# A new order for the start and the first pair of a hashed attention with two expert layers behind it

## The chip, the cores and the metric

The kernel runs on one core of a Trainium2 chip. The metric is the device time of one execution in microseconds (us). TensorE (PE) has two levels of clock here, 1.2 and 2.4 GHz. The other engines are VectorE (DVE), ScalarE (ACT), GpSimd (POOL) and SyncE, whose queue (SP) issues nearly all DMAs.

## The reference

All arrays are float32. An attention over 2 batches, 8 heads, 768 tokens and head dimension 64 keeps only the keys whose hash bucket equals the query's; a soft mixture of 8 experts follows, and then a layer of 2048 hidden units.

```python
q_bits = (np.einsum('bhsd,dk->bhsk', q, proj) > 0)      # 6 bits, a bucket of 0..63; k the same
mask = q_bucket[:, :, :, None] == k_bucket[:, :, None, :]
scores = np.where(mask, scale * np.matmul(q, k.transpose(0, 1, 3, 2)), -1e9)
scores = scores - np.max(scores, axis=-1, keepdims=True)
attn = np.exp(scores); attn = attn / (np.sum(attn, -1, keepdims=True) + 1e-9)
x = np.matmul(attn, v)                                  # heads joined: 1536 tokens x 512
...
logits = x @ phi                                        # 32 slots: dispatch over tokens, 8 experts, combine
...
h = x @ w_in; g = h - np.tanh(h); out = g @ w_out
```

## The kernel before, in words

Two heads make a pair, and there are eight pairs. The work of a pair is cut into small units, and each unit issues a few instructions on several engines. Every engine takes its instructions strictly in the order in which the units are written out, so the lists of unit names below are the schedule. `START` (line 66) is the order of what comes ahead of the first pair; `STEP` (line 71) is gone through once for each of pairs 0 to 6, `LAST` (line 74) for pair 7. In `START` a name carries its pair after the dot. In a step of pair i, the table `role` (line 678) adds an offset: `m`, `l`, `g`, `f`, `d`, `v` and `v1`, `v2` work on pair i+1, `h`, `b` on pair i+2, `qk` on i+3, the score units `s0`, `s1` and `a` on pair i itself.

The units that matter here:

- `const.0`, `const.1`, `const.2` load constants: `ct` on the SP queue; the small `blk` on SP and the hash matrix `projb` on ACT's queue; `phiB` in two DMAs on SP. `qk` loads a pair's queries and keys (xq, xk), `v` its values (tv).
- `bq`, `bk` (lines 349 to 357): the hash bits of queries or keys, matrix products `pb` on PE and comparisons `bt` on DVE. `wq0v`, `wk0a`, `wq1p` and so on (line 359) write rows made of the bits beside the operands QA, KA; the last letter says the engine (v DVE, a ACT, p POOL, s a part on ACT and a part on DVE).
- `h0` to `h3` (`hp` on POOL): the rounded high part of keys and queries into KA, QA. `l0` to `l3`: the low part into KB, QB. For pair 0 the low parts are subtractions on POOL (lines 426 to 433). For later pairs `g` copies the high part to PSUM on ACT (line 407, tile hp) and `l` subtracts it on DVE (line 416). `d` copies the high parts into the other halves of QB, KB by DMA.
- `m` (line 437), 18 for a pair: masked scores `pm` on PE, and the maximum over keys of them on DVE (`mx`, line 446). `fa`, `fb` (one head each) and `f2` (both) transpose the maxima (`mh`, `pc` on PE, `zrow`, `row` on DVE) and send them by DMA into QA; `fz` sends the flags of empty rows (zrw).
- `s0`, `s1` (line 497), nine for each head: the scores `pst` on PE (line 503), the exponential `e` on ACT (line 505), and for most a running sum `es` on POOL (line 515). `a` (line 520) is the product of `e` of both heads and the values, `pav` on PE.
- `v1`, `v2`: sums of the values (va on POOL, pv on PE, vt on DVE, vhi on ACT, vn and vzw on POOL).
- `wl`, `wc` (lines 629, 638): load a piece of the third layer's weight and convert it: one `cg` on ACT and three operations on DVE (lines 183, 192, 197, the middle one needs `cg`). At most two pieces are loaded and not converted; a `wc` with nothing loaded does nothing.
- `keep.n` and `warm.4`: small products on PE whose results nobody uses. `oi` clears rows of operands (on POOL, and once on DVE).

PSUM tiles of all these units come from one pool of six, `ps` (line 270).

After the pairs, the expert layer's weights stream in on SP as buffers come free (`load_pieces`, called at fixed places of pairs 5 to 7), and the last layer follows in an order of its own (`MOE`, `RUN`, `LOOP`).

Of the kernel before, what the change touches and what calls it, by code (L numbers as in the profile page):

```python
# [25 lines left out]
NPR = B * H // 2  # L26
# [36 lines left out]

START = ("warm.4 const.1 qk.0 const.0 hp2.0 keep.1 oi.0 const.2 h0.0 bk.0 bq.0 keep.3 wq0v.0 kc.0 wl.0 keep.3 wk0a.0 "
# [3 lines left out]
        "keep.1 oi.2 wl.0").split()  # L70
STEP = ("a a a m xe s0 g1 m a m l1 s1 s0 s1 m s0 m m g0 l0 m xr s1 h1 m m s0 m a m m wl m g2 s1 lp l2 s0 v wl a d m wc "
        "lp v1 e m s0 s0 a wl a lp a e s1 lp m m h0 s1 s0 qk m v2 h3 s1 e lp a f2 lp b s0 x2 e fz wc s1 wc s1 lg lp h2 "
        "x3 a a wl lp").split()
LAST = ("a a s0 a lp xe a a a s0 lp lp a a lp s0 s0 lp s0 s1 s1 s0 s1 xr s0 s1 s1 lp s1 s1 lp a a lp a s0 x2 s1 s0 lg "
        "x3 s1 a").split()
# [57 lines left out]
def body(ctx: ExitStack, tc: tile.TileContext, q, k, v, proj, phi, w1, w2, w_in, w_out, cst, out, dbg=None):  # L133
    nc = tc.nc
    const = ctx.enter_context(tc.tile_pool(name="const", bufs=1))
# [6 lines left out]
    lg = const.tile([P, B * KT, NS], F32, name="lg")  # L142
# [78 lines left out]
    def open_ring(n, stack, side="right"):  # L221
        for _ in range(n):
            slots.append(stack.enter_context(tc.tile_pool(name=f"ring{len(slots)}", bufs=1, side=side, reuse_waits="tile")))
# [10 lines left out]
    def load_pieces(n):  # L234
        for _ in range(n):
            t = n_loaded[0]
            if t >= NPC or t >= len(slots) < NSLOT:
                return
            n_loaded[0] += 1
            which, e, half = pieces[t]  # L240
            w = slot_tile(slot_of(t), F32R if which == 4 else F32, "w")
            if which != 4:
                src = w_out.bitcast(U32)[e] if which == 3 else (w1, w2)[which - 1][e, half]
                nc.sync.dma_start(out=w.rearrange("p a n -> p (a n)").bitcast(src.dtype), in_=src)
            w_t[pieces[t]] = w


    def attention():
# [31 lines left out]
        last = NPR - 1  # L280
# [348 lines left out]
        def win_load():  # L629
            n = win_n[0]  # L630
            if n < 16 and len(raws) < 2:
                win_n[0] += 1
                c, fq = n // 4, n % 4
                raw = cv.tile([P, 1024], U32, tag="raw", name="raw")
                nc.sync.dma_start(out=raw, in_=win_v[:, c, fq * 1024:(fq + 1) * 1024])
                raws.append((raw, c, fq))

        def win_cvt():
            if raws:
                raw, c, fq = raws.pop(0)  # L640
                g = cv.tile([P, 512], F32, tag="cg", name="cg")
                l = psum("cl")[:, :512].bitcast(U32)
                cvt_b(cvt_a(raw, g, l), win[:, c, fq * 512:(fq + 1) * 512])
# [96 lines left out]
        nc.vector.memset(wz, 0.0)  # L740
        for w in START:
            u, n = w.split(".")
            unit(u, int(n))
        del wt[:]
        for i in range(NPR):
            for u in STEP if i < NPR - 1 else LAST:
                n = i + role.get(u, role.get(u[0], 0))
                if 0 <= n < NPR:
                    unit(u, n)
                if i == 5 and not slots and 6 not in xqs and 6 not in xks:  # L750
                    while raws or win_n[0] < 16:
                        win_load()
                        win_cvt()
                    raw_x.close()
                    open_ring(RING[0], rctx)
                if i == 6 and len(slots) == sum(RING[:2]) and not xqs and not xks:
                    xq_x.close()
                    open_ring(RING[2], rctx)
                if i == last and half.get((i, 0)) == len(SEQ) and len(slots) == sum(RING[:4]) and not xtu and last in pav:
                    head_x.close()  # L760
                    load_pieces(RING[3])
                    open_ring(RING[4], rctx)
                    load_pieces(RING[4])
                if i == last and half.get((i, 1)) == len(SEQ) and len(slots) == sum(RING[:5]):
                    last_x.close()
                    open_ring(RING[5], rctx)
                    load_pieces(RING[5])
            if i == 5:
                mid_x.close()
                open_ring(RING[1], rctx)  # L770
            if i == 6:
                early_x.close()
                load_pieces(RING[1] + RING[2])
                open_ring(RING[3], rctx)
        last = NPR - 1
# [549 lines left out]

    with tc.manual_schedule():
        attention()
        if dbg is not None and "lg" in dbg:
            nc.sync.dma_start(out=dbg["lg"], in_=lg)
# [70 lines left out]
```

## Time and profile before

| what | us |
|---|---|
| runs of the kernel, lowest, median, highest | 464.77, 465.33, 466.93 |
| the profiled execution, its time | 464.5 |
| its span, first to last instruction | 462.7 |
| busy: PE, DVE, ACT, POOL | 442.7, 330.5, 271.8, 289.3 |

The time of an execution holds 1.8 us outside the span. Busy PE counts matmuls whose ends are modelled, and the products of `keep` too. The order of the units is read off on each engine: an idle time that a row names belongs to the instruction that comes next in the list.

### The profile page before, as it was taken

The page shows a single profiled execution, that of the slowest core. Times are in us where ns is not written, and L with a number is a line of the kernel's source. Part 1 is how long each engine was busy: PE and PEld are TensorE (multiplying, and loading weights), DVE is VectorE, ACT ScalarE, POOL GpSimd, SP SyncE. Part 2 cuts the span into 40 slices and gives each one's busy share as a digit, 9 for nine tenths or more (in the row PEclk, how much of TensorE's full clock was granted, in tenths as well). Part 3 has the DMA queues.
Part 4 walks back from the last instruction along what each step waited for, and adds up shares of the span by engine and source line. Part 5 has one row for each costly group of instructions (what it writes and reads, how often), then busy time and mean ns, then how long its engine had stood idle before and what let it go on. Part 6 is the DMA issues. An engine that isn't in the chain of part 4 may idle for free. (4 is left out here: it accounts for less than half of the span.)

```text
span 462.7 us, 7587 instructions
## 1 busy us (share of the span) xinstructions
PE 442.7 (96%) x2639; PEld 296.6 (64%) x2639; DVE 330.5 (71%) x592; ACT 271.8 (59%) x521; POOL 289.3 (63%) x291
## 2 busy tenths in 40 slices
PE   7589999999999999999999999999999999999995
PEld 3455565656666575766765544567777778888883
DVE  3999798897989969577173438579998976544441
ACT  4526676756776565654450111278889887666661
POOL 4976977889697896958871110025888884444450
PEclk9889999999999999999999999999999999999998
DMA  6337337153633509449539999992000003000004
GB/s 195 110 98 221 125 98 219 41 170 127 189 125 106 167 15 298 178 142 326 216 157 379 421 416 417 419 419 83 2 1 2 0 0 137 1 1 1 0 1 144
DMA packets 18342, 71.32 MB, mean 154 GB/s; under 512 B 3668, under 2 KB 4792, under 8 KB 13176
## 3 DMA queue, kind: packets, MB, share of 16 engines
q1 hardware_dynamic: 17976, 70.75, 43.5%
q8 instruction: 23, 0.38, 0.4%
q14 instruction: 23, 0.19, 0.1%
q10 hardware_dynamic: 320, 0.01, 0.0%
HBM read 60.08 MB, written 3.15 MB: 137 GB/s over the span
## 5 line engine op out<-in xcount | busy, mean ns | idle before, releaser
L505 ACT ACTIVATE e<-pst 128x512 f32<-128x512 f32 x144 | 79.9, 598 | 44.6 <-PE pst L503 40.9
L515 POOL TENSOR_TENSOR es<-es,e 128x512 f32<-128x512 f32 x73 | 92.9, 1288 | 13.1 <-ACT e L505 13.0
L446 DVE TENSOR_REDUCE mx<-pm 128x1 f32<-128x512 f32 x144 | 90.2, 682 | 10.7 <-PE pm L444 9.8
L532 PE MATMUL pav<-e,tv 128*64 128x512 f32 (+1 forms) x384 | 70.5, 496 | 0.0
L503 PE MATMUL pst<-QA,KA 128*128 128x256 f32 (+1 forms) x192 | 67.7, 367 | 0.8 <-DVE mx L446 0.4
L503 PE MATMUL pst<-QB,KB 128*128 128x256 f32 (+1 forms) x192 | 62.2, 338 | 0.0
L1221 DVE SCALAR_TENSOR_TENSOR ph<-win,ph 128x512 f32<-128x512 f32 (+1 forms) x64 | 35.7, 558 | 32.2 <-ACT win L1216 30.8
L444 PE MATMUL pm<-KA,QA 96*128 96x512 f32 x192 | 51.5, 369 | 2.8 <-DVE QA L368 2.4
L1252 POOL TENSOR_TENSOR split<-win,split 128x512 fp32r<-128x512 f32 x31 | 44.8, 1447 | 14.2 <-ACT split L1247 14.2
L1273 PE MATMUL po<-w,split 128*128 128x512 f32 x128 | 51.0, 399 | 0.0
L1271 PE MATMUL po<-w,split 128*128 128x512 f32 x128 | 50.6, 396 | 0.0
L515 POOL TENSOR_TENSOR es<-e 128x512 f32<-128x512 f32 x30 | 39.2, 1316 | 18.1 <-PE pr L546 18.0
L1272 PE MATMUL po<-w,split 128*128 128x512 f32 x128 | 50.5, 394 | 0.0
L444 PEld LDWEIGHTS pm<-KA,QA 96*128 96x128 f32 x192 | 34.0, 197 | 24.1 <-ACT e L505 7.3
L503 PEld LDWEIGHTS pst<-QA,KA 128*128 128x128 f32 x192 | 36.1, 188 | 20.2 <-DVE mx L446 7.1
L1252 POOL TENSOR_TENSOR ghl<-win,ghl 128x256 fp32r<-128x256 f32 x32 | 24.2, 757 | 37.0 <-ACT ghl L1247 37.0
L1216 ACT ACTIVATE win<-ph 128x512 f32<-128x512 f32 (+1 forms) x64 | 30.8, 481 | 23.0 <-PE ph L1209 22.3
L1222 DVE SCALAR_TENSOR_TENSOR win<-win,ph 128x512 f32<-128x512 f32 (+1 forms) x64 | 35.5, 555 | 8.7 <-DVE ph L1221 0.5
L532 PEld LDWEIGHTS pav<-e,tv 128*64 128x64 f32 x384 | 24.1, 136 | 27.1 <-issue 20.4
L1217 ACT ACTIVATE win<-win,ct 128x512 f32<-128x512 f32 (+1 forms) x64 | 39.5, 617 | 2.1
L503 PEld LDWEIGHTS pst<-QB,KB 128*128 128x128 f32 x192 | 36.4, 189 | 2.0
L1273 PEld LDWEIGHTS po<-w,split 128*128 128x128 f32 x128 | 24.0, 188 | 7.7 <-POOL split L1252 2.7
(236 smaller groups left out, 818.4 us busy)
## 6 DMA issues: line engine op xcount, KB each, us to landing
w<-in_moe_w_dram SPq DMA_DIRECT2D x32, 1024.0 KB
raw<-in_moe_w_in_dram SPq DMA_DIRECT2D x16, 512.0 KB
w<-in_moe_w_out_dram SPq DMA_DIRECT2D x8, 1024.0 KB
xq<-in_q_dram SPq DMA_DIRECT2D x8, 384.0 KB
xk<-in_k_dram SPq DMA_DIRECT2D x8, 384.0 KB
tv<-in_v_dram SPq DMA_DIRECT2D x8, 384.0 KB
out_dram<-win SPq DMA_DIRECT2D x12, 256.0 KB
QB<-QA SPq DMA_DIRECT2D x10, 192.0 KB
```

What stands on the lines that cost most here:

```text
L444: nc.tensor.matmul(pm[:, j * 256:j * 256 + c1 - c0], QA[s][h][:96, c * P:(c + 1) * P], KA[s][h][:96, c0:c1], start=True, stop=True)
L446: nc.vector.reduce_max(m, pm.rearrange("p (c k) -> p c k", c=len(cs)), axis=AX.X)
L503: nc.tensor.matmul(pst[:, j * 256:j * 256 + c1 - c0], K[h][:, c * P:(c + 1) * P], Q[h][:, c0:c1], start=x == 0, stop=x == 1)
L505: nc.scalar.activation(e, pst, AF.Exp, scale=0.125)
L515: eng.tensor_tensor(q[0], y, e, ALU.add)
L532: nc.tensor.matmul(pav[i][k][64 * h:64 * h + 64, :], tv[i][:, h, c, :], e2[h][:, j * 256:j * 256 + c1 - c0], start=False, stop=c == KT - 1 ...
L1217: nc.scalar.activation(w, z, AF.Square, bias=ct[:, C_QA:C_QA + 1])
L1221: nc.vector.scalar_tensor_tensor(self.ph[p], z, Q_C, self.ph[p], ALU.mult, ALU.mult)
L1252: (eng or nc.gpsimd).tensor_tensor(gl[p], g, gh[p].bitcast(F32), ALU.subtract)
L1271: nc.tensor.matmul(po, gh[p][:, us], wo.half(f, 0), start=f == 0, stop=False)
L1272: nc.tensor.matmul(po, gh[p][:, us], wo.half(f, 1), start=False, stop=False)
L1273: nc.tensor.matmul(po, gl[p][:, us], wo.half(f, 0), start=False, stop=f == NF - 1)
```

## The change

Three things are edited, all of them orders. `START` is a new list. It holds the old one's units and six `s0.0`, the first six score units of the first head of pair 0, near its end; there are 9 products of `keep` fewer (14 for 23). The first pair goes through a list of its own, `FIRST`, which is `STEP` with six `s0` fewer and another order.

```diff
-START = ("warm.4 const.1 qk.0 const.0 hp2.0 keep.1 oi.0 const.2 h0.0 bk.0 bq.0 keep.3 wq0v.0 kc.0 wl.0 keep.3 wk0a.0 "
-        "h1.0 wq1a.0 keep.1 qk.1 keep.1 hp3.0 wl.0 m.0 m.0 m.0 keep.1 m.0 m.0 m.0 wk1a.0 m.0 m.0 m.0 h3.1 h2.1 h1.1 "
-        "v.0 fa.0 m.0 m.0 m.0 m.0 l1.0 m.0 m.0 m.0 oi.1 m.0 m.0 wl.0 keep.1 keep.3 v.1 v1.0 wc.0 bq.1 d.0 bk.1 l0.0 "
-        "fb.0 l2.0 l3.0 h0.1 wq1p.1 wq0p.1 v2.0 keep.3 wk0v.1 fz.0 keep.3 keep.2 kc.1 a.0 qk.2 wc.0 wc.0 wk1a.1 "
-        "keep.1 oi.2 wl.0").split()
+START = ("qk.0 warm.4 const.0 const.2 const.1 wl.0 hp2.0 oi.0 bk.0 keep.1 h0.0 wl.0 keep.3 keep.3 bq.0 kc.0 wq0v.0 "
+        "wk0a.0 h1.0 keep.1 hp3.0 m.0 keep.1 m.0 qk.1 v.0 m.0 m.0 m.0 wk1a.0 h1.1 wq1a.0 keep.1 m.0 m.0 h3.1 m.0 d.0 "
+        "h2.1 m.0 m.0 m.0 fa.0 m.0 m.0 m.0 l1.0 m.0 m.0 m.0 oi.1 l0.0 m.0 keep.1 wl.0 v.1 keep.3 l3.0 bq.1 v1.0 bk.1 "
+        "wq1p.1 wc.0 wq0p.1 v2.0 s0.0 fb.0 l2.0 wk0v.1 h0.1 s0.0 wc.0 s0.0 a.0 s0.0 wc.0 oi.2 wl.0 s0.0 fz.0 wk1a.1 "
+        "kc.1 s0.0 qk.2").split()
+FIRST = ("a g1 a m m a m l1 xe a s1 xr m s1 m m m g0 m h1 s1 l0 a m m wl v1 m m d m g2 l2 a s1 v lp wl m h0 a lp wc a wl "
+        "lp e m s0 a m qk lp m s1 e s0 s1 m s0 v2 h3 s1 lp f2 e lp b a fz wc s1 s1 lg lp e x3 h2 a a wl x2 lp wc").split()
 STEP = ("a a a m xe s0 g1 m a m l1 s1 s0 s1 m s0 m m g0 l0 m xr s1 h1 m m s0 m a m m wl m g2 s1 lp l2 s0 v wl a d m wc "
         "lp v1 e m s0 s0 a wl a lp a e s1 lp m m h0 s1 s0 qk m v2 h3 s1 e lp a f2 lp b s0 x2 e fz wc s1 wc s1 lg lp h2 "
         "x3 a a wl lp").split()
...
-            for u in STEP if i < NPR - 1 else LAST:
+            for u in FIRST if i == 0 else STEP if i < last else LAST:
```

A unit whose pair does not exist, an `a` without both exponentials, and a `wc` or `wl` that has nothing to do issue nothing. The effective changes of order in `START` are these. The loads of xq, xk go ahead of `blk`, and two pieces of weight go ahead of `qk.1`. `bk.0` stands ahead of the first `keep`. `fa.0` stands behind eleven `m.0` and not nine, `d.0` ahead of it. Behind the last `m.0`, both hash units `bq.1`, `bk.1` stand ahead of the first `wc` and not behind it; then come `v2.0`, the first `s0.0` and `fb.0`, which was ahead of `v2.0`. On ACT the order behind `vhi` (of `v2.0`) is now: e, h0.1, e, cg, e, e, e, the rows of `wk1a.1`, e, and then `g1.1` of the first pair. It was: cg, `wk1a.1`, e, `g1.1`.

## Rows read from the trace of the kernel before

**Rows 1.** Busy time of each engine in stretches: the start, steps 0 and 1.
```profile
8.20:34.85 26.65, 18.44 (x92) 12.71 (x90) 23.89 (x44) 11.14 (x18) 21.41 (x25) 0.87 0.41 131
34.85:60.27 25.42, 24.43 (x129) 14.22 (x130) 22.80 (x42) 17.71 (x32) 21.54 (x21) 1.00 0.54 160
60.27:87.83 27.56, 27.56 (x167) 17.18 (x166) 24.76 (x47) 18.57 (x34) 22.34 (x22) 1.00 0.48 137
```
**Rows 2.** The timeline of DVE, start of the kernel to the first pair.
```profile
11.27 2.36 DVE L368 TENSOR_SCALAR QA<-bt,ct 24x512 fp32r<-24x512 f32 x2
...
26.11 0.68 DVE L183 TENSOR_SCALAR cl<-raw 128x512 uint32<-128x512 uint32 x1
...
28.34 1.97 DVE L357 TENSOR_SCALAR bt<-pb 24x512 f32<-24x512 f32 x4
30.32 0.17 DVE L451 TENSOR_REDUCE mh<-mx 128x6 f32<-128x12 f32 x1
...
31.46 0.27 DVE L490 TENSOR_TENSOR vt<-pv,blk 4x128 f32<-4x128 f32 x1
31.77 0.91 DVE L368 TENSOR_SCALAR KA<-bt,ct 24x512 fp32r<-24x512 f32 x2
...
34.85 1.88 DVE L446 TENSOR_REDUCE mx<-pm 128x1 f32<-128x512 f32 x3
36.64 1.37 DVE L416 TENSOR_TENSOR QB<-xq,hp 64x512 fp32r<-64x512 f32 x2
```
**Rows 3.** The timeline of DVE, end of step 0.
```profile
56.81 0.70 DVE L192 SCALAR_TENSOR_TENSOR cl<-cg,cl 128x512 uint32<-128x512 uint32 x1 [1.23 <-ACT cg L179]
...
58.93 0.70 DVE L192 SCALAR_TENSOR_TENSOR cl<-cg,cl 128x512 uint32<-128x512 uint32 x1
...
60.27 1.36 DVE L446 TENSOR_REDUCE mx<-pm 128x1 f32<-128x512 f32 x2
```
**Rows 4.** Busy time of each engine, 250 to 310 us; the last two columns are DMA share and GB/s.
```profile
250.00:310.00 60.00, 57.47 (x562) 31.02 (x560) 35.66 (x66) 13.93 (x33) 5.27 (x14) 1.00 1.01 419
```
**Rows 5.** The timeline of the SP queue, its first issue.
```profile
0.73 0.39 SPq L168 DMA_DIRECT2D blk<-in_const_dram  x1
```
**Rows 6.** The timeline of PE, start and early step 0.
```profile
19.77 0.37 PE L454 MATMUL pc<-ct,mh 128*6 128x128 f32 x1 [3.37 <-DVE mh L451]
...
24.89 1.06 PE L355 MATMUL pb<-xq,projb 128*32 128x512 f32 x1
...
25.74 1.43 PE L355 MATMUL pb<-xq,projb 128*32 128x512 f32 x3
...
34.98 0.50 PE L503 MATMUL pst<-QA,KA 128*128 128x512 f32 x1 [0.40 <-DVE win L197]
...
36.16 0.40 PE L503 MATMUL pst<-QA,KA 128*128 128x512 f32 x1
...
36.62 0.39 PE L444 MATMUL pm<-KA,QA 96*128 96x512 f32 x1
```
**Rows 7.** The timeline of ACT, end of the start and early step 0.
```profile
31.77 0.31 ACT L491 ACTIVATE vhi<-vt 4x128 fp32r<-4x128 f32 x1 [14.38 <-DVE vt L490]
31.98 0.65 ACT L179 ACTIVATE cg<-raw 128x512 f32<-128x512 f32 x1
32.66 1.29 ACT L366 ACTIVATE KA<-bt,ct 24x512 fp32r<-24x512 f32 x2
...
34.77 0.60 ACT L407 ACTIVATE hp<-xq 128x512 fp32r<-128x512 f32 x1
35.76 2.44 ACT L505 ACTIVATE e<-pst 128x512 f32<-128x512 f32 x4 [0.38 <-PE pst L503]
...
39.63 0.83 ACT L378 ACTIVATE QA<-xq 64x768 fp32r<-64x768 f32 x1
```
**Rows 8.** The timeline of POOL, the first subtraction.
```profile
11.23 1.79 POOL L428 TENSOR_TENSOR QB<-xq,QA 64x768 fp32r<-64x768 f32 x1 [1.28 <-ACT QA L378]
```
**Rows 9.** Busy time of each engine in the stretch of the low clock.
```profile
19.70:26.50 6.80, 6.73 (x23) 4.85 (x24) 6.28 (x12) 0.00 (x0) 4.54 (x4) 0.50 0.53 149
```

## The prediction

> **What bounds the kernel now.** The page shows PE as the busiest engine, so PE seems to be the bound. The stretches say otherwise for the place of the change. From 8.20 to 34.85 us, the start, DVE is busy 23.89 of 26.65 us and PE only 18.44, with useless `keep` products among them; in step 0, to 60.27, PE is busy 24.43 of 25.42 and DVE 22.80; the next step takes 27.56 [rows 1]. The reader is to see that PE and DVE are both nearly full in step 0, so the timeline has to decide. It does: the maxima of pair 1 begin on DVE at 34.85, at 36.64 comes the subtraction of `l1.1`, and from there DVE's rows follow each other with little between them up to 60.27, where the maxima of pair 2 begin [rows 2, 3]. The one long gap is 1.23 us before a conversion, for `cg` of ACT [rows 3]. I take DVE's chain as what sets the begin of step 1, and so I follow DVE's time through the new order. What step 1 begins later or earlier is passed on whole: the steps behind it keep their order, and the stream of expert weights, which fills the DMA from 250 to 310 us (a share of 1.01, 419 GB/s) [rows 4], starts at fixed places of that order and so moves with it.
>
> **The change part by part.** DVE's instructions are the same in number and size, in the start and in step 0; only waits and order differ. PE loses 9 `keep` in the start, and six score units move from step 0 into the start. Such a unit takes PE 0.46 us (36.16 to 36.62) [rows 5] and ACT 0.61 (2.44 for four) [rows 6], so step 0 is lighter by 2.8 us on PE and 3.7 on ACT. That is worth nothing as long as DVE is the last to be ready.
>
> 1. *First loads.* The issue of `blk`, 0.39 us, no longer stands ahead of xq and xk [rows 7], and bits of keys no longer wait behind a `keep`. All that DVE does may begin up to 0.45 us earlier; it may also be nothing, since the hash matrix comes by ACT's queue, whose order stays. I take -0.25. `blk` is late, but is not read before vt.
>
> 2. *Hash bits ahead of the conversion.* Behind the last maximum DVE goes on at 26.11 with a conversion (2.23 us, to 28.34), and only then with the four comparisons (1.98, to 30.32) [rows 2]. The conversion covers the bits on PE: the first product's two passes begin at 24.89 and 25.74, 0.85 us apart [rows 5], so its result stands at about 26.6. In the new order DVE wants it at 26.11 - 0.25 = 25.86. At the low clock of 0.50, which PE has from 19.70 to 26.50 [rows 8], DVE waits some 0.65 us, and up to 1.3 if the keys' bits are late as well; at the full clock passes take half, and it waits for nothing. I take half of 0.65, +0.3.
>
> 3. *vt moves ahead of `fb`.* In the old order vt began at 31.46, behind the transposition of the maxima (1.14 us, from 30.32) [rows 2]. In the new one it follows the conversion: 25.86 + 1.98 + 0.3 + 2.23 = 30.37.
>
> 4. *The queue of ACT behind vt.* This is the step on which the forecast rests. ACT waits for vt with vhi (14.38 us of idle time end there) [rows 6], and all exponentials moved into the start are queued behind vhi. Ahead of the hp that `l1.1` subtracts there stand now vhi 0.31, six e of 0.60, h0.1 0.83, cg 0.65, the rows of `wk1a.1` 1.29, and hp itself takes 0.60: 7.28 us [rows 6]. vhi begins 0.31 behind vt (31.46 to 31.77) [rows 2, 6]. So hp ends at 30.37 + 0.31 + 7.28 = 37.96, and DVE's subtraction starts at 38.0 where it was 36.64: +1.35. In the old order only one e stood there, hp ended at 35.37 [rows 6], and DVE did not wait for it. Queued behind the subtraction on DVE are fifteen maxima and everything else of step 0.
>
> 5. *DVE's own way to the same place.* From vt: 1.14 for `fb`, 3.39 for rows and conversion (31.46 to 34.85), three maxima 1.79 (34.85 to 36.64) [rows 2], and perhaps a wait in which PE makes the first score of pair 1 in the PSUM tile that the conversion has just left. The old order has such a wait, at 34.98 for the conversion's last operation, and the product took 0.50 [rows 5]; I put 0.6. That is 30.37 + 6.92 = 37.3. ACT is later by 0.7, so this wait costs nothing; if ACT were not last, the loss would still be 0.65.
>
> 6. *The end of step 0.* The 1.23 us for `cg` [rows 3] become less: the first `cg` stands ahead of one more e, so it comes 0.6 earlier. But the second one now has two e and one h ahead of it, 0.65 + 1.2 + 0.83 = 2.7 us behind the first, and DVE asks for it 2.12 behind (56.81 to 58.93) [rows 3]. The 0.6 won are lost again: 0, with bounds of -0.6 and +0.6.
>
> The sums `es` of the moved units go into POOL's queue behind the last low part; POOL has 3.9 us free in step 0 [rows 1] and is relieved there: nothing. The DMAs of `d.0` go from behind `fa`'s to ahead of it on SP, which had been idle; the low part that needed them waits less, on POOL: nothing on DVE. Two pieces of weight ahead of `qk.1` delay xq of pair 1, which ACT reads early in the start, and ACT has 14.38 us free behind it [rows 6]: nothing.
>
> The sum: 1.35 + 0 (term 6) and 0.15 for small new waits (score units of step 0 that want hp's PSUM tile, which is left 1.35 later) gives +1.5 us. On the profiled execution that is 464.5 + 1.5 = 466.0 (span 462.7 + 1.5 = 464.2, and 1.8 around it). The median of the runs, 465.33, lies 0.8 above that execution, so the forecast for the median is 466.8.
>
> **A price that a port sets.** The two row writes of the start take DVE 2.36 us at 11.27, the same two later 0.91 at 31.77 [rows 2]; during the first pair POOL's subtraction runs, from 11.23 for 1.79 us [rows 9], begun 0.04 us ahead of DVE's. If DVE came first, it would save up to 1.45 us. The Trainium skill says in "SBUF — State Buffer", section "SBUF: two separate sides", that DVE in its two-port modes and GpSimd share one pair of ports, and that whichever starts first holds it for its whole instruction while the other is blocked. By that rule the sum would be the same or 1.45 less, decided by some hundredths of a microsecond; the trace agrees as far as one such meeting can.
>
> **The rivals.** *PE sets the end of step 0 (faster).* Then the six units are worth 6 x 0.46 = 2.8 us, which gives 465.3 - 2.8 = 462.5. For it speaks that PE is busy 96% of step 0 [rows 1]; against it, that DVE's maxima follow each other without idle time there. It decides if DVE waits for PE for more than about 2 us of step 0, so that PE's relief comes to the front.
>
> *The port falls to DVE.* The likeliest case with -1.45: 465.3. The start's first comparisons and POOL's subtraction both move with the keys' bits, so the tie of 0.04 us mostly stays lost.
>
> *The chain of ACT is hidden*, because vt is earlier than I think or ACT's rows overlap: term 5 is left, and 466.0 or a little less comes out, down to 465.3 if its 0.6 is not waited for.
>
> *The low clock lasts into step 0 (slower).* After PE has stood idle for 3.37 us before a transposition, the clock is at 0.50, that is 1.2 GHz, for 6.80 us [rows 5, 8]. The new order takes away the `keep` products that stood before step 0, and between the first `s0.0` and the transposition of `fb` PE has nothing to do for 2 to 5 us (the bits end 2 us or more before vt). If the clock then falls for another 6.8 us, PE does 3.4 us less work in that stretch, of which its idle 1.0 us of step 0 [rows 1] hides a part: about +2.4, so 469.2. It decides if the low clock reaches past the begin of pair 1's maxima.
>
> **How the numbers follow.** The likeliest case, ACT's chain, has 0.45; alone it runs from 465.8 to 468.0, by the bounds of terms 1, 2 and 6. The port or a hidden chain, both near 465.3 to 466.0, have 0.23. PE as the bound has 0.12, the low clock 0.20. Half a per cent, 2.3 us, is about what a measurement of this kernel can tell from no change: 463.0 to 467.7. Faster by more than that is the case of PE, 0.12. Slower by more is the low clock and the upper end of the likeliest case, 0.20 + 0.07 = 0.27. The rest is 0.61. The range leaves out most of PE's case and the tail of the low clock: 463.6 to 469.2.
>
> **What would show it.** In the changed profile: on DVE, the first `l1.1` subtraction (line 416) at about 38.0 us, with idle time before it that ends with hp of ACT; vt at about 30.4, with a wait of 0 to 1.3 us before the comparisons behind the last maximum of pair 0; the first maximum of pair 2 near 61.8; steps of 27.56 us behind it. ACT without idle time between vhi and hp. If DVE's subtraction does not wait for hp, term 4 is wrong; if the maxima of step 0 wait for PE again and again, DVE was not the bound, or the clock was low, which the granted clock tells; if the first pair of row writes takes 0.9 us, the port fell to DVE. The prediction fails most simply if DVE has much less to wait for in step 0 than now.

## The result and the profile after

In the same rounds the changed kernel took 466.99 us (median of 20 runs, 465.25 to 473.65) and the kernel before 464.93 (20 runs, 462.11 to 466.93); the ratio is 1.006, 95% interval 1.004 to 1.008. So the change costs time. The forecast of 466.8 is met within 0.2 us; the loss of 0.6% by the ratio (0.44% by these medians) is more than the 0.3% that the forecast made of it against its own median. One of the 20 runs, 473.65 us at a granted clock of 0.929, is a slow one and is left out of the ratio; without it the median is 466.88. The profiled execution took 468.85 us, with a span of 466.7: 4.0 over that of before.

The other 19 runs lie in two groups, eleven from 465.25 to 467.10 us and eight from 468.85 to 470.60. Of the 20 of before, three lie at 462.11 to 462.35 and the rest from 464.10 on. The profiled execution of the changed kernel belongs to its upper group, so its timeline adds up to the loss of that group and not to that of the median.

The row numbers in the prediction are from 5 on not those of the headings. Where it says rows 5, 6, 7, 8, 9 it means the groups headed Rows 6 (PE), Rows 7 (ACT), Rows 5 (SP queue), Rows 9 (the low clock), Rows 8 (POOL). Rows 1 to 4 are right. From here on the numbers are those of the headings.

The stretches of the changed kernel: the start, steps 0 and 1, the stretch of the low clock, and the stream of expert weights. The columns are those of rows 1: start and end, length, busy time and number of instructions of PE, of PE's weight loads, of DVE, ACT and POOL, then the granted clock, the DMA share and GB/s.

```profile
7.86:37.90 30.04, 21.69 (x83) 13.26 (x78) 25.95 (x44) 13.58 (x22) 21.82 (x25) 0.77 0.47 139
37.90:63.41 25.51, 22.48 (x115) 12.02 (x116) 22.89 (x41) 15.91 (x28) 23.04 (x22) 1.00 0.48 138
63.41:91.00 27.59, 27.59 (x167) 17.23 (x166) 24.78 (x46) 18.50 (x34) 20.96 (x22) 1.00 0.48 137
...
13.20:26.90 13.70, 11.77 (x39) 7.84 (x40) 12.48 (x22) 4.38 (x6) 10.33 (x12) 0.50 0.51 145
...
253.30:313.30 60.00, 57.61 (x561) 31.00 (x560) 35.69 (x65) 13.95 (x33) 5.29 (x14) 1.00 1.01 419
```

Against [rows 1, 4, 9]: step 0 lasts 25.51 where it lasted 25.42, although PE has 2 us less to do in it; step 1 is what it was; the stream is the same, 3.3 us later. Nearly all of it arose in the start: 30.04 us from the first comparison to the first maximum of pair 1, where it took 26.65, begun 0.35 earlier. And PE has the low clock for 13.7 us, not 6.8.

The timeline of DVE says where. The start, with the end of step 0 below:

```profile
11.27 2.66 DVE L370 TENSOR_SCALAR QA<-bt,ct 24x512 fp32r<-24x512 f32 x2
13.96 0.69 DVE L448 TENSOR_REDUCE mx<-pm 128x1 f32<-128x512 f32 x1
15.07 6.25 DVE L448 TENSOR_REDUCE mx<-pm 128x1 f32<-128x512 f32 x10 [0.42 <-PE pm L446]
...
27.42 1.03 DVE L359 TENSOR_SCALAR bt<-pb 24x512 f32<-24x512 f32 x2 [0.57 <-PE pb L357]
28.71 1.02 DVE L359 TENSOR_SCALAR bt<-pb 24x512 f32<-24x512 f32 x2 [0.26 <-PE pb L357]
...
31.77 0.27 DVE L492 TENSOR_TENSOR vt<-pv,blk 4x128 f32<-4x128 f32 x1
...
33.19 2.55 DVE L370 TENSOR_SCALAR KA<-bt,ct 24x512 fp32r<-24x512 f32 x2
...
37.90 1.88 DVE L448 TENSOR_REDUCE mx<-pm 128x1 f32<-128x512 f32 x3
39.70 1.37 DVE L418 TENSOR_TENSOR QB<-xq,hp 64x512 fp32r<-64x512 f32 x2
...
59.15 0.70 DVE L194 SCALAR_TENSOR_TENSOR cl<-cg,cl 128x512 uint32<-128x512 uint32 x1 [0.72 <-ACT cg L181]
...
61.70 0.70 DVE L194 SCALAR_TENSOR_TENSOR cl<-cg,cl 128x512 uint32<-128x512 uint32 x1 [0.52 <-ACT cg L181]
...
63.41 2.00 DVE L448 TENSOR_REDUCE mx<-pm 128x1 f32<-128x512 f32 x3 [0.29 <-PE pm L446]
```

POOL, ACT, PE and the SP queue beside it, of the same execution, a fence for each:

```profile
10.88 1.79 POOL L430 TENSOR_TENSOR QB<-xq,QA 64x768 fp32r<-64x768 f32 x1 [1.47 <-ACT QA L380]
...
33.68 1.90 POOL L432 TENSOR_TENSOR KB<-xk,kh 64x768 fp32r<-64x768 f32 x1
```
```profile
32.08 0.31 ACT L493 ACTIVATE vhi<-vt 4x128 fp32r<-4x128 f32 x1 [13.34 <-DVE vt L492]
...
38.02 0.60 ACT L409 ACTIVATE hp<-xq 128x512 fp32r<-128x512 f32 x1
```
```profile
13.10 0.64 PE L446 MATMUL pm<-KA,QA 96*128 96x512 f32 x1 [2.50 <-DVE QA L370]
...
35.20 1.41 PE L446 MATMUL pm<-KA,QA 96*128 96x512 f32 x4 [0.35 <-issue]
...
38.04 0.50 PE L505 MATMUL pst<-QA,KA 128*128 128x512 f32 x1 [1.42 <-DVE win L199]
```
```profile
0.73 0.39 SPq L322 DMA_DIRECT2D xq<-in_q_dram  x1
...
6.28 0.55 SPq L170 DMA_DIRECT2D blk<-in_const_dram  x1
```

The first maximum of pair 0 comes at 13.96 us in both kernels; that of pair 1 at 37.90 against 34.85 [rows 2]: +3.05. Three pieces make it. The eighteen maxima of pair 0 end 0.66 later (26.85 against 26.19), because they wait for PE; most of that is PE's clock, which falls to 0.50 at 13.2 us instead of 19.7 (0.14 stays where it falls late, see the products of `keep` below). The comparisons behind them wait 0.57 and 0.26 for the bits. And the two row writes at 33.19 take 2.55 us, where they took 0.91 [rows 2]: 1.64 more, while POOL's subtraction `l2.0` (33.68, 1.90 us) runs. The first of the two still took 0.71; the second took 1.92. In the kernel before `l2.0` was over long ahead of that write, on POOL:

```profile
22.73 1.81 POOL L430 TENSOR_TENSOR KB<-xk,kh 64x768 fp32r<-64x768 f32 x1
```

The rest of the way from vt to the maxima is the transposition of `fb`, which only changed its place. The three sum to 3.13; the exchanges of order around them give back the last 0.08.

The span grew by another 0.94 us far from the change: from the first product of the last layer's hidden part to its last takes 143.87 us, and it took 142.93. A conversion on DVE at 348.66 lasts 1.47 us beside POOL's product at 348.56, and PE later waits for POOL:

```profile
348.66 1.47 DVE L185 TENSOR_SCALAR win<-w 128x512 uint32<-128x512 uint32 x1
```
```profile
353.54 0.50 PE L1275 MATMUL po<-w,split 128*128 128x512 f32 x1 [0.76 <-POOL split L1254]
```

In the kernel before DVE began that conversion 0.22 us ahead of the same product (345.09 and 345.31) and took 0.56; here the product is 0.10 ahead. All fourteen profiled executions of this study have one of these two lengths, 142.90 to 142.95 or 143.87 to 143.96; the kernel before with only its score units moved (below) has the longer one too. What chooses between them is open.

### The profile page after: what moved, and what is told of

Same layout as the page of the kernel before. It is cut to its first block, busy times and chain, and to the rows that moved or that the text cites. A ratio compares the mean times of both kernels' runs of the same rounds, so it can differ in the third digit from the quotient of the medians.

```text
span 466.7 us, 7556 instructions
## 1 busy us (share of the span) xinstructions
PE 444.1 (95%) x2621; PEld 295.9 (63%) x2621; DVE 333.4 (71%) x592; ACT 272.4 (58%) x521; POOL 288.8 (62%) x291
## 5 line engine op out<-in xcount | busy, mean ns | idle before, releaser
L517 POOL TENSOR_TENSOR es<-es,e 128x512 f32<-128x512 f32 x73 | 93.1, 1289 | 12.1 <-ACT e L507 11.8
L446 PE MATMUL pm<-KA,QA 96*128 96x512 f32 x192 | 53.9, 383 | 3.6 <-DVE QA L370 2.5
```

Source lines behind the costliest of these rows:

```text
L446: nc.tensor.matmul(pm[:, j * 256:j * 256 + c1 - c0], QA[s][h][:96, c * P:(c + 1) * P], KA[s][h][:96, c0:c1], start=True, stop=True)
L517: eng.tensor_tensor(q[0], y, e, ALU.add)
```

## The experiments

Every kernel differs from the one named by a few names in `START`. "First to first" is the time from the first maximum of pair 0 to that of pair 2 on DVE's timeline of the profiled execution: 46.31 us before (13.96 to 60.27 [rows 2, 3]), 49.45 after. It leaves out when the first rows of the kernel are ready, which differs between executions.

**The changed kernel again.** Nothing is edited.

> The changed kernel once more, nothing edited, for how much its timeline differs from execution to execution. Port theory: DVE's rows of wk0v.1 meet POOL's subtraction of l2.0 again and take 2.55 us, first maximum of pair 1 at 37.9 us, first maximum of pair 2 at 63.4. Clock theory: if the clock falls late (near 20 us and not 13), the first maximum of pair 1 comes some 0.7 us earlier. Time 467 against 465 of before.

469.54 us (6 runs, 466.12 to 471.5), ratio to before 1.011 (1.006 to 1.016); first to first 49.47, the rows again 0.71 and 1.91. The held write repeats to a hundredth. The rest does so less closely: the maxima of pair 0 take 13.08 us, first to last, where they took 12.89, and the bits are waited for 0.67 where it was 0.83.

**POOL's `l2.0` ahead of its rows.** The meeting of the row write with `l2.0` is taken away.

> The changed kernel with l2.0 moved from behind fb.0 to behind v1.0, into 4.27 us that POOL has free. Port theory: the two rows of wk0v.1 fall from 2.55 to 0.91 us and the first maximum of pair 1 comes 1.6 us earlier, at 36.3. If my forecast's theory of ACT's queue holds beside it, the first l1.1 subtraction then waits for hp (which ended at 38.62) and begins at about 38.7 where it was 39.70, so that only 1.0 us is gained by pair 2; without that theory 1.6 us. Rival, the rows are long for another reason than POOL: 2.55 stays and nothing moves.

```diff
-... v1.0 bk.1 wq1p.1 wc.0 wq0p.1 v2.0 s0.0 fb.0 l2.0 wk0v.1 ...
+... v1.0 l2.0 bk.1 wq1p.1 wc.0 wq0p.1 v2.0 s0.0 fb.0 wk0v.1 ...
```

`l2.0` runs at 24.16, while DVE does maxima. DVE and ACT in this kernel:

```profile
33.24 1.02 DVE L370 TENSOR_SCALAR KA<-bt,ct 24x512 fp32r<-24x512 f32 x2
...
36.42 1.88 DVE L448 TENSOR_REDUCE mx<-pm 128x1 f32<-128x512 f32 x3
38.69 1.38 DVE L418 TENSOR_TENSOR QB<-xq,hp 64x512 fp32r<-64x512 f32 x2 [0.39 <-ACT hp L409]
```
```profile
38.06 0.60 ACT L409 ACTIVATE hp<-xq 128x512 fp32r<-128x512 f32 x1
```

The writes take 1.02 (0.70 and 0.40, overlapping): the meeting was the cause of the 1.64. But now `l1.1` waits for hp of ACT: DVE stands idle for 0.39, hp ends at 38.66, and `l1.1` begins at 38.69. That is the wait on which the forecast rested; in the changed kernel DVE was so late that it could not be seen. Time 467.84 (463.13 to 469.06), ratio 1.0036 (1.0003 to 1.0068); first to first 49.38. From vt to `l1.1` it takes 1.05 less than in the changed kernel, as expected with ACT's queue next. Two other things of this execution take the gain back: the bits were waited for 1.41 us in all, where it was 0.83, and the clock was low once more in step 0, which took 0.5 longer from `l1.1` on:

```profile
37.90:44.70 6.80, 6.61 (x18) 3.95 (x18) 6.22 (x10) 3.81 (x8) 6.66 (x6) 0.50 0.84 234
```

**The products of `keep` back behind the bits.** Only this stretch of PE is as it was before.

> The changed kernel with the six useless products of two keep.3 put back behind bq.0, where the old order has them; the seven ahead of bq.0 stay. Clock theory: PE then is active up to the first maxima's scores as it was, the clock stays at 1.00 past 13 us and falls near 20 us as before, and the eighteen maxima of pair 0 end 0.7 us earlier (26.1 and not 26.85). Rival, the moment when the clock falls comes from how the execution happens to lie: it falls near 13 us here too, or near 20 us in the repeated changed kernel as well.

```diff
-... bq.0 kc.0 ...
+... bq.0 keep.3 keep.3 kc.0 ...
```

The clock falls at 19.3 and not at 13.2, and stays low for 6.8 us; the maxima of pair 0 take 12.37 us, first to last, where they took 12.89 (12.23 before). The bits are waited for (0.62 and 0.26) and the row writes take 2.54 as in the changed kernel. First to first 48.99; time 467.29 (465.68 to 469.26), ratio 1.006 (1.003 to 1.009). So 0.5 us of the loss hung on the clock in this execution, and the bigger part did not.

**Before, with only the six score units moved.** The order of before, and six `s0.0` at the end of `START`.

> The kernel before with nothing changed but six s0.0 written at the end of its START (its STEP then has six s0 that issue nothing). PE theory (the six units are worth 2.8 us because PE sets the end of step 0): the first maximum of pair 2 comes at 57.5 and the kernel takes 462. DVE theory: DVE's order is that of before, the first maximum of pair 1 is at 34.9, but six exponentials stand ahead of hp on ACT: hp ends at 34.15 + 6 x 0.6 + 0.6 = 38.4 and l1.1 waits until then (it began at 36.64), so the first maximum of pair 2 comes 1 to 1.8 us later than 60.27, and the kernel takes 466.

```diff
-... wk1a.1 keep.1 oi.2 wl.0
+... wk1a.1 keep.1 oi.2 wl.0 s0.0 s0.0 s0.0 s0.0 s0.0 s0.0
```

DVE and ACT:

```profile
34.02 0.69 DVE L197 SCALAR_TENSOR_TENSOR win<-raw,cl 128x512 uint32<-128x512 uint32 x1
36.27 1.99 DVE L446 TENSOR_REDUCE mx<-pm 128x1 f32<-128x512 f32 x3 [1.56 <-PE pm L444]
38.18 1.37 DVE L416 TENSOR_TENSOR QB<-xq,hp 64x512 fp32r<-64x512 f32 x2
```
```profile
33.77 3.63 ACT L505 ACTIVATE e<-pst 128x512 f32<-128x512 f32 x7
37.42 0.60 ACT L407 ACTIVATE hp<-xq 128x512 fp32r<-128x512 f32 x1
```

Relief for PE in step 0 gains next to nothing (from `l1.1` to the first maximum of pair 2 it takes 23.50 us, where it took 23.62): `l1.1` comes at 38.18 where it came at 36.64, and first to first is 47.94, 1.6 over before. The moved work delays what stands behind it where it is moved to, in two queues: on PE it stands ahead of the first masked scores, for which DVE waits 1.56; on ACT it puts off hp to 38.02, which would hold `l1.1` at the same place if PE did not. 467.53 us (466.05 to 469.71), ratio 1.007 (1.004 to 1.010).

**The conversion first, as before.** In the changed kernel `wc.0` stands ahead of `bq.1` again, so that it covers the bits.

> The changed kernel with the first wc.0 put back ahead of bq.1. Cover theory: the comparisons behind the last maximum of pair 0 do not wait for PE (the changed kernel waited 0.57 and 0.26 us there), so that from the last maximum's end to vt it takes 4.1 to 4.3 us where it took 4.9, and the first maximum of pair 1 comes 0.8 us earlier than 37.9 at an equal clock. The rows of wk0v.1 still meet POOL's subtraction and take 2.5 us. Rival, the waits are PE's queue and not its lateness: they come back at another place and the 4.9 us stay.

```diff
-... l3.0 bq.1 v1.0 bk.1 wq1p.1 wc.0 wq0p.1 ...
+... l3.0 wc.0 bq.1 v1.0 bk.1 wq1p.1 wq0p.1 ...
```

```profile
25.61 1.97 DVE L359 TENSOR_SCALAR bt<-pb 24x512 f32<-24x512 f32 x4
27.61 0.28 DVE L492 TENSOR_TENSOR vt<-pv,blk 4x128 f32<-4x128 f32 x1
...
34.50 1.38 DVE L418 TENSOR_TENSOR QB<-xq,hp 64x512 fp32r<-64x512 f32 x2 [0.51 <-ACT hp L409]
```

No wait for the bits: vt 4.15 us behind the last maximum, where it was 4.92. Against the expectation the row writes were over before POOL came to `l2.0` (30.70), so they took 0.92, and `l1.1` waits for hp again. First to first 47.63. The profiled execution has a span of only 461.7, and yet the median is 467.08 (463.76 to 468.35), ratio 1.005 (1.002 to 1.008): its first maximum of pair 0 came at 10.61 and not at 13.96, which not every execution has. Two things make it. DVE's very first row writes went ahead of POOL's subtraction (9.41 against 10.08) and took 0.86, not 2.66. And they could begin 1.85 us earlier, because PE made the bits faster: the two passes of the first product begin 0.43 us apart, in the changed kernel 0.82, although the granted clock is recorded as 1.00 in both stretches. PE here, and in the changed kernel:

```profile
6.01 0.59 PE L357 MATMUL pb<-xk,projb 128*32 128x512 f32 x1 [1.21 <-DMA projb<-in_proj_dram]
...
6.44 0.59 PE L357 MATMUL pb<-xk,projb 128*32 128x512 f32 x1
```
```profile
5.94 1.03 PE L357 MATMUL pb<-xk,projb 128*32 128x512 f32 x1 [1.14 <-DMA projb<-in_proj_dram]
...
6.76 1.06 PE L357 MATMUL pb<-xk,projb 128*32 128x512 f32 x1
```

Three of the fourteen profiled executions have the short passes in all of the first bits; what chooses is not shown.

**All three edits together.**

> The changed kernel with three edits undone together: l2.0 early, keep.3 keep.3 behind bq.0, the first wc.0 ahead of bq.1. If these three are the loss on DVE, the last maximum of pair 0 ends at 26.0, vt is at 30.2, the rows take 0.9 us and the first maximum of pair 1 is at 34.7, where before had 34.85. ACT's queue is then what is left: hp ends 6.9 us behind vt, at 37.0, l1.1 waits for it, and the first maximum of pair 2 is at 60.7 (before 60.27). Time within 1 us of before. Rival, something else of the new order costs time too: 61.5 or later for pair 2.

466.23 us (463.61 to 468.03), ratio 1.0038 (1.000 to 1.008). vt again 4.15 behind the last maximum, row writes 0.86, `l1.1` waits for hp (0.56). Its first bits were made at the quicker pace as well, and the first maximum of pair 0 came at 10.60. First to first is 49.02, where the expectation comes to 46.7 (60.7 less 13.96): the clock was low at 15.1 to 25.4, so that the maxima of pair 0 took 13.4 us, and at 49.3 to 52.7; the stretch from `l1.1` to the first maximum of pair 2 took 24.53 where it takes 23.73 at the full clock.

**And ACT's conversion ahead of the exponentials.** The fourth cause is taken away too: `g1.1`, which makes hp, behind `h0.1`.

> The kernel of the three edits, and g1.1 written in START behind h0.1, so that hp stands on ACT ahead of five of the six moved exponentials. Theory of ACT's queue: hp ends near 32, l1.1 begins when DVE gets there, at 36.5, and the first maximum of pair 2 is at 60.2, 0.5 us ahead of the kernel of the three edits. Rival, l1.1 is held by something else than hp, or the PSUM tile that hp then occupies longer delays the score units: no gain, or pair 2 later than 60.7.

```diff
-... wk0v.1 h0.1 s0.0 wc.0 ...
+... wk0v.1 h0.1 g1.1 s0.0 wc.0 ...
```

```profile
33.88 0.70 DVE L194 SCALAR_TENSOR_TENSOR cl<-cg,cl 128x512 uint32<-128x512 uint32 x1 [0.40 <-ACT cg L181]
...
37.01 1.37 DVE L418 TENSOR_TENSOR QB<-xq,hp 64x512 fp32r<-64x512 f32 x2
```
```profile
32.21 0.57 ACT L409 ACTIVATE hp<-xq 128x512 fp32r<-128x512 f32 x1
```

`l1.1` no longer waits; hp is done at 32.78. The conversion of the weight waits 0.40 for its `cg`, which is now behind hp. First to first 46.80, still 0.49 over before, time 464.72 (461.94 to 465.94), ratio 0.9987 (0.9956 to 1.0017). With its four hindrances removed the new order is as good as the old one, and not measurably better.

**The first rows on ACT.** In five kernels the pair 0 rows that DVE writes are given to ACT (`wq0v.0` becomes `wq0a.0`, behind `h1.0`), so that the meeting at 11.3 us does not take place. First this alone on the kernel above, then, in one set on one chip, on before, on before with the score units moved, on the changed kernel, and on that with `l2.0` early.

> The kernel before this one, with the first rows of queries (wq0v.0, on DVE, 1.9 to 2.7 us beside POOL's subtraction) written by ACT behind h1.0 (1.29 us), where POOL cannot hold them up. Port theory: the first score of pair 0 begins near 12.5 us and not 13.1 to 13.5, its first maximum near 13.0 and not 13.6 to 14.0, and all that follows is 0.7 to 1.0 us earlier, the first maximum of pair 2 at 59.4: the first version here that beats both, by 1 us. Rival, another operand or the scores on PE are late as well: nothing is gained.

> The kernel before, with the head's first row writes given from VectorE to ScalarE, so that which of VectorE and GpSimd writes first at the first rows no longer decides the time of pair 0. First maximum of pair 0 near 12.7 us, first maximum of pair 2 some 46.5 later, at about 59.2. Time about 463.8 us with its runs within some 1.5 us of each other, if the first rows make most of the spread of the kernel before; about 465 and as wide as before if they don't.

> The order of before with only the first pair's six score units moved ahead, and the first rows on ScalarE. If ScalarE's queue behind the conversion of pair 1 is what the move costs, l1.1 waits for ScalarE's conversion and the first maximum of pair 2 comes some 47.9 us after that of pair 0: 1.4 to 1.6 us over the kernel before with the same rows. If TensorE's relief in step 0 counted, 2.8 us under it.

> The changed kernel with the first rows on ScalarE. The port meeting of VectorE's row write with GpSimd's l2.0, the early fall of the clock and the waits for the bits stay: 49.4 us from the first maximum of pair 0 to that of pair 2, near 62.1; time some 3 us over the kernel before with the same rows. If the cost of the change was only a matter of which engine came first at the first rows, within 1 us of it.

> The changed kernel with GpSimd's l2.0 issued ahead of its two row subtractions of pair 1, and the first rows on ScalarE. VectorE's second row write falls from 1.9 to 0.4 us. If ScalarE's queue decides next, l1.1 waits for ScalarE's conversion and the time is about 1.0 us under the changed kernel with the same rows; if the port was the whole loss, 1.6 or more under it.

| with the first rows on ACT | median of 12 (range), us | first to first, us | span, us |
|---|---|---|---|
| four edits (earlier set) | 464.03 (463.37 to 464.41) | 46.57 | 462.0 |
| before | 463.6 (462.82 to 467.14) | 46.80 | 461.7 |
| before, score units moved | 464.69 (463.92 to 467.04) | 47.72 | 463.0 |
| changed kernel | 465.99 (465.20 to 467.38) | 49.30 | 464.3 |
| changed kernel, `l2.0` early | 464.37 (463.92 to 466.10) | 48.91 | 463.4 |

Ratios to before, in the order of the table: 0.9986 (0.9959 to 1.0012), 0.9991 (0.9958 to 1.0023), 1.0013 (0.9985 to 1.0040), 1.0025 (0.9999 to 1.0051), 1.0004 (0.9979 to 1.0030). None beats before beyond its interval, which had been expected of the four edits. They spread over 1.0 us, where the same kernel with these rows on DVE ran from 461.94 to 465.94 and the kernel before from 461.36 to 467.94 beside them (35 runs): so the first rows make much of the spread. But three of before's twelve with this edit lie at 465.16 to 467.14, away from the other nine, so not all of it.

Between the lower four, by medians: the moved units alone cost 1.1 us, the whole change 2.4 (3 was expected), and of these 1.6 are gone when `l2.0` no longer meets the row write. Drawing the twelve runs of each anew gives 95% ranges of -0.1 to 3.2, 1.3 to 3.2 and 0.6 to 2.3: the second and third are clear of noise, the first is not. In the earlier set the moved units cost 2.5 by medians, but that kernel's profile has the longer last layer, which no kernel with these rows on ACT has. The 1.6 lies above the 1.0 that was expected if ACT's queue came next, but the range holds both. The changed kernel of this set shows the other pieces apart. DVE, and the stretches from `l1.1` to the first maximum of pair 2 and of the low clock inside it:

```profile
24.64 2.11 DVE L359 TENSOR_SCALAR bt<-pb 24x512 f32<-24x512 f32 x4
...
30.20 2.54 DVE L370 TENSOR_SCALAR KA<-bt,ct 24x512 fp32r<-24x512 f32 x2
```
```profile
36.70:61.77 25.07, 22.12 (x110) 11.72 (x109) 21.22 (x38) 14.42 (x25) 22.12 (x22) 0.93 0.44 130
...
50.90:54.30 3.40, 3.40 (x18) 2.60 (x20) 2.40 (x7) 2.04 (x4) 3.40 (x4) 0.50 0.80 258
```

Here the clock was full at the bits, and DVE hardly waited for them (2.11 us for the four, 1.97 without any wait), although their order is that of the changed kernel; the expectation of an early fall was wrong for this execution (it came at 20.2). The port was met all the same, 2.54 us. And the clock fell inside step 0, which took 25.07 us from `l1.1` on, 1.34 more than at the full clock. PE had then waited 1.06 us for DVE's conversion ahead of 50.49. In the kernel with `l2.0` early `l1.1` does wait for hp again, which ends at 36.51 (`l1.1` at 36.55, an idle time of 0.39), and from vt to `l1.1` it takes 6.88 us against 7.92. So ACT's queue came next and the meeting cost 1.0 at this place, as expected. The profiles differ otherwise too, in the clock above all: with `l2.0` early it fell at 11.4, and first to first is only 0.4 shorter. Where the other 0.6 of the medians comes from, if it is not noise, is open.

## Why the time was right and the reason only in part

The forecast for the median, +1.5 us, met +2.1; in the profiled execution the terms summed to +1.5 and the first maximum of pair 2 came 3.14 later (63.41 against 60.27; forecast 61.8). So the figure was helped by chance: the median of before lay 0.4 above its profiled execution (464.93 and 464.5), that of after 1.9 below (466.99 and 468.85). If the two groups of runs of either kernel correspond, which no run shows, the change costs about 4 us in each (medians 469.2 against 465.1, and 466.0 against 462.2); the median shows 2.1 because the changed kernel is in its lower group in 11 of 19 runs and before in 3 of 20. By the steps of the prediction:

1. *First loads, -0.25: 0.* The first bits came 0.35 earlier (7.86 against 8.21), but the queries' bits at 10.21 in both, so the rows of pair 0 began at 11.27 as before; they took 2.66 where they took 2.36, behind POOL's subtraction. The first maximum did not move.
2. *Bits ahead of the conversion, +0.3: +0.83.* The mechanism is as told, a wait for PE that depends on the clock: 0.57 and 0.26 at the low clock, nothing at the full clock, nothing with the conversion back in front. The bounds of 0 to 1.3 held. That the clock would fall at 13.2, which makes some 0.5 of the 0.66 by which the maxima are later, is in no term.
3. *vt at 30.37: 31.77.* The terms above make the 1.4: the maxima end 0.99 later than 25.86, the comparisons wait 0.53 more than assumed, and the rest is taken back. In the changed kernel with ACT's rows vt is 4.17 behind the last maximum, against 5.27 with before's order: that vt moves ahead by the length of `fb` is right.
4. *ACT's queue.* hp ended at 38.62, 6.85 behind vt; forecast 7.59. The sum took ACT's instructions one behind the other, but most of them begin 0.09 before the one ahead ends, and five of the six e took 0.57 and not 0.60. And DVE came to `l1.1` only at 39.70, so nobody waited, and by the prediction's own test the step on which it rested was wrong in this kernel. The kernels in which the row write was quick and hp still behind the exponentials show it in its place: `l1.1` starts 0.03 us behind the end of hp with `l2.0` early (twice), with the conversion first, and with all three edits, and 0.15 behind it in the two with the units alone, where PE was late as well; with hp ahead of the exponentials it does not wait. The time from vt to `l1.1` sums it up: 7.92 or 7.93 us in the four executions whose row write met `l2.0`; 6.88 to 6.90 in the four where it did not and hp stands behind the exponentials; 6.55 in the two with hp ahead. So ACT's queue is worth 0.34 over DVE's own way, where the forecast had 0.7, and the meeting 1.04 over ACT's queue.
5. *DVE's own way, 6.92 from vt to `l1.1`: 7.93.* This is the step that failed. It took the row writes at the 0.91 of [rows 2], and weighed POOL's hold on them at the start only. In the new list `l2.0` stands right ahead of `wk0v.1`, and both become free together behind vt and `fb`: the second write took 1.92 us. The 0.6 for a PSUM tile did not come: PE had made the first masked scores at 35.20, and DVE went from one to the next.
6. *End of step 0, 0:* the waits for `cg` are 0.72 and 0.52, 1.24 in all, against 1.23 [rows 3]. Right.

*The port.* At 11.27 POOL was ahead, by 0.39 where it had been 0.04, so that rival fell as the text said it mostly would. POOL's `l2.0` began at 33.68, inside the first row write, and the second one, begun at 33.82, ended at 35.73, just behind `l2.0` (35.58). The Trainium skill says in "SBUF — State Buffer", section "SBUF: two separate sides", that of a GpSimd instruction and one of DVE in a two-port mode the one that starts first holds the shared ports for its whole instruction; the trace agrees, at a place where the prediction had not applied it.

*PE sets the end of step 0.* Refuted: with the units moved alone, first to first got 1.6 us longer, not 2.8 shorter. *ACT's chain hidden.* So it was, by the port and not by an early vt; its price of 0.65 for DVE's own way was then too low by the port.

*The low clock in step 0.* Not in the changed kernel's profile, whose step 0 has 1.00 throughout, but in four of the ten executions with the order `FIRST`, for 3.4 or 6.8 us; at most it cost 1.34 (25.07 against 23.73), where 2.4 was priced. The runs do not separate what part of the medians it makes. Of the first fall of the clock it is open, too, whether the fewer `keep` bring it on. In the six executions with the order `FIRST` and without the six products of `keep` put back it came at 11.4, 11.8, 13.2, 13.6, 14.0 and, with ACT's rows, 20.2 us; in the four with them back at 15.1, 19.3, 19.9 and 20.2. So it mostly comes later with them, but not always, and what decides is not shown.

## What to carry to other kernels

Work moved ahead of a bottleneck delays what stands behind it in every queue that it enters (six units alone put hp off from 35.38 to 38.02); ask on each engine what stands behind it there, before asking what is relieved where it was. When an order is changed, list the pairs of DVE and POOL instructions that become free at the same moment, as for a clash of addresses: a write of 0.45 us became one of 1.92 by a neighbour that the old order had 9 us earlier (22.73 to 31.77). And where two engines race for something at the start, look at the spread before the median: one kernel's runs lay within 4.0 us of each other with such a race and within 1.0 without it.

## What the runs showed of the hardware that was not expected

- DVE's row write that begins beside a running subtraction of POOL ends only when POOL is done, at two separate places of the kernel: at the second it took 1.91 or 1.92 us in the four executions in which `l2.0` was ahead of it, and 0.40 or 0.45 in all others. Being first with the first of two writes does not help the second: in the kernel before with its units moved DVE began at 11.34, POOL at 11.74, and DVE's second write still took 1.91.
- PE's first products have two paces, with passes 0.43 or 0.82 us apart at a recorded granted clock of 1.00, and so the queries' bits came at 8.35 to 8.42 us in three of the ten executions of the new order and at 9.85 to 10.63 in the others.
- The length of the last layer has two values, 1.0 us apart, in executions whose order there is the same. In seven of the eight longer ones one DVE conversion lasted 1.46 or 1.47 us beside POOL; the five kernels with the first rows on ACT all had the shorter. What links them was not tried.
